# fc2 by seven block products in both halves of the tokens, from the first half's 7th group on

## The chip, the cores and the metric

One core of one Trainium2 chip runs the whole kernel. The metric is device time in microseconds (us), the median of several runs. Five engines matter: PE (TensorE) multiplies matrices, DVE (VectorE), ACT (ScalarE) and POOL (GpSimd) do elementwise work, SP (SyncE) issues the DMA transfers. Each engine works off its own instructions strictly in the order in which the program emits them.

## The reference

A transformer block on 2048 tokens of width D = 576, with an adaptive modulation (`sa, ca, ga, sb, cb, gb`) computed from a small vector `c`. Only its second half is touched by the change:

```python
x = x + ga * attention(layernorm(x) * (1 + ca) + sa)        # 32 query heads, one key/value head
h = layernorm(x) * (1 + cb) + sb
y = layernorm(h)                                            # the "second norm" of the MLP
x = x + gb * (gelu(y @ w1 + b1) @ w2 + b2)                  # w1: 576 x 4608, w2: 4608 x 576
```

All arithmetic is float32. The kernel gets it from float32r matmuls: each operand is split in a high part (a rounded copy) and a low part (operand minus high part), and a product is high times high, high times low, low times high.

## The kernel before

The attention runs first and ends at about 1430 us. Then the MLP runs in 36 *groups*, numbered v = 0 to 35 in the code's loop `for v in range(NV)`. A group takes 256 of the 4608 hidden channels for half of the tokens: v = 0 to 17 are the first *pair* of token blocks (tokens 0 to 1023), v = 18 to 35 the second pair (tokens 1024 to 2047). Tiles are 128 tokens; `XT[:, t, :]` is the residual of tile t, which is also the accumulator of the output.

In each group, fc1 is done by seven block products in the manner of Strassen and Winograd (`product`, L1042: A11, S2, S3, A12, S1, A22, S4, in this order). Each has its weights in `W1["r"]` and its input pieces in `OP`, which `op_pieces` forms from the normed and transposed activations `YR[pair]`. Weight sums for the groups that aren't precomputed (3 to 16) are formed during the first pair by `w1_part`, `w1_sum` and `tail_parts`, one group ahead, mostly on POOL, then saved to DRAM for the second pair.

fc1 gives four activation blocks per group. `gelu` (L1057) evaluates each on ACT, makes the high part on ACT (L1060) and the low part on POOL (L1061). The order in a group is A22, A11, A21, A12 in the names that fc2 uses for them; A21 is not split when fc2 goes by seven products.

fc2 differs between the pairs.

- First pair (`fc2`, L1153): 96 matmuls of 128x288 per group, 12 for each of 8 token tiles, and one DVE addition into `XT` per tile (L1157).
- Second pair, groups 18 to 34 (`fc2s`, L1122): seven block products, 12 matmuls each, 84 in all, in the order of `SEVEN`: S3, A22, A11, A12, S2, S1, S4. `sums` forms S3, S2, S1, S4 from the gelu results on POOL (L1098 the difference, L1095 the high part, L1096 the low part). Each product is followed by two DVE additions (L1128), into `XT` or into a spare accumulator `eb`, which POOL adds in at the end (L1136). The last group, 35, is plain.

fc2 of group v runs while fc1 of group v+1 does, one product between two fc1 products (`t_()` steps the generator). In the seven-product groups there are seven such places per group; the first place after the boundary holds the last product (S4) of the group before last, and S3 of the last group has the second place, behind fc1's A11 and S2. Only in the first group after the switch is the first place left out.

At the end of a group the program emits, in this order: fc1's S4 and its DVE addition (L1299); the last gelu's activation; one fc2 product with its two DVE additions; the weight sum S4 and `tail_parts` (L773 to L776, POOL) where weights are formed; then the first step of `sums`, which makes S3. After the boundary: fc1's A11, the ACT copy of it to `U` (L1230), then the last gelu's split (L1060, L1061), then the second step of `sums`, and so on.

The second norm of token blocks 2 and 3 (`ln2_tile`, eight tiles) is spread in small steps over groups 2 to 16 of the first pair (`more`, at seven places in each group).

Of the kernel before, what the change touches and what calls it, by code (L numbers as in the profile page):

```python
# [18 lines left out]
KD = 5  # L19
# [4 lines left out]
NG = F // 256  # L24
R3 = 3 * DH
# [5 lines left out]
def block_kernel(ctx: ExitStack, tc, x, wqkv, wo, w1, b1, w2, b2, c, wmod, ident_in, out):  # L31
# [34 lines left out]
    w2sum = dr.tile([NG, 128, 4, 2, 288], F32, name="w2sum")  # L66
    qscr = dr.tile([NB, 2, H * DH, TB], F32, name="qscr")
# [453 lines left out]
    def ln2_tile(tb, t):  # L521
# [15 lines left out]
        e = po if fine else ve  # L537
        e.tensor_scalar(h, X, mv[:, 0:1], rs, op0=ALU.subtract, op1=ALU.mult)
# [16 lines left out]
        if fine:
            yield
# [17 lines left out]
    def ln2_block(tb):  # L574
        if "b" not in B2:
            B2["b"] = b2_scaled(load_b2())
        if tb % 2 == 0:
            YR[tb // 2] = per.tile([128, 2 * KD, TB], F32, name="yr", tag="big", bufs=3)
        for t in range(NT):
            yield from ln2_tile(tb, t)  # L580
        if tb % 2:
            R = YR[tb // 2]
            po.tensor_tensor(R[:, 5:7], R[:, 7:9], R[:, 5:7], op=ALU.subtract)
            yield
            po.tensor_tensor(R[:, 5:7], R[:, 5:7], R[:, 0:2], op=ALU.add)
            yield
# [100 lines left out]
    def weight_parts():  # L687
# [283 lines left out]
    W2, W2S, GT = [], [], []  # L971

    def wo_end():
# [8 lines left out]
        W1["pool"] = tc.tile_pool(name="mr", bufs=1, reuse_waits="tile")  # L982
        mr = W1["pool"].__enter__()
# [3 lines left out]
        load_w2(0)  # L987

# [19 lines left out]
    def w1_sum(w):  # L1008

        o, a = W1["s"], 4 * OPS.index(w)  # L1010
        def op(x, y, how=ALU.subtract):
            po.tensor_tensor(o, x, y, op=how)
# [9 lines left out]
        po.tensor_copy(W1["r"][:, a:a + 2], o)  # L1022
# [3 lines left out]

    def load_w2(v, to=None):
        for l in range(2):
            sy.dma_start((to or W2[v % 2])[l].bitcast(F32), w2scr[v % NG, :, l])
# [14 lines left out]

    G = {(-2, 1, 0): 0, (-1, 0, 0): 1, (-1, 0, 1): 2, (-1, 1, 1): 3, (-1, 1, 0): 4}

    def gelu(v, f, b, p):

        if v < NG:
# [3 lines left out]
        else:  # L1053
            u = G[v, b, f] = GU["A%d%d" % (2 - b, 2 - f)][v % 2] if v == NV - 1 or (b, f) != (0, 1) else None
            h = YR[1][:, 2 * b + f, :]
        ft = 2 * (v % NG) + f
# [16 lines left out]
    def xb(b, nn, j):  # L1073

        return XT[:, 2 * NT + NT * (1 - b) + 2 * j:, 288 * nn:288 * (nn + 1)][:, :2]

    def eb(j):
# [9 lines left out]

    def sums(v):

        h = [[YR[1][:, 3 - 2 * i - j, :] for j in range(2)] for i in range(2)]  # L1090
        s1, s2, s3 = (YR[1][:, i, :] for i in (4, 5, 6))

        def parts(w, x):
            u = GU[w][v % 2]
            po.tensor_copy(unit(u, 0), x)  # L1095
            po.tensor_tensor(unit(u, 1), x, unit(u, 0).bitcast(F32), op=ALU.subtract)  # L1096

        po.tensor_tensor(s3, h[0][0], h[1][0], op=ALU.subtract)  # L1098
        parts("S3", s3)
        yield  # L1100
        po.tensor_tensor(s1, h[1][0], h[1][1], op=ALU.add)
        po.tensor_tensor(s2, s1, h[0][0], op=ALU.subtract)
# [4 lines left out]
        po.tensor_tensor(s3, h[0][1], s2, op=ALU.subtract)  # L1107
        parts("S4", s3)

    def fc2s(v):  # L1110

        bank = []
        for k, (w, first, to) in enumerate(SEVEN):
            gh, gl = (unit(GU[w][v % 2], l) for l in range(2))
            for j in range(2):
# [8 lines left out]
                o = eb(j) if to is None else xb(*to, j)  # L1124
                if v == NG and k == 2:
# [3 lines left out]
            if v + 2 < NV:  # L1129
                load_w2s((v + 1) % NG, k)  # L1130
            else:
                if k == 3:
                    load_w2(NV - 1, W2[0])
                for to in ((), (), (), (), ((1, 0),), ((1, 1),), ((0, 1),))[k]:
                    for j in range(2):
                        po.tensor_tensor(xb(*to, j), xb(*to, j), eb(j), op=ALU.add)  # L1136
# [3 lines left out]
    def fc2(v):  # L1140
        h2, l2 = W2[v % 2 if v < NG else 0]
        for bt in range(2 * NT):
# [15 lines left out]
            if v % NG == NG - 1:  # L1158
# [3 lines left out]
    fill = deque([ln2_block(2), ln2_block(3)])  # L1162
# [17 lines left out]
    mark = [None]  # L1180

    for v in range(NV):
        nxt = (v + 1) % NG
        if v == NG - 1:
            while fill:
                step(fill)
            form = op_pieces(YR[1], po)

        def more(half="", first="", room=False):
# [3 lines left out]
            elif 1 < v < NG and fill and (room or mark[0] != "T") and half not in ("-T3 -B21", "=T4 +t0"):  # L1193
                mark[0] = next(fill[0], "end")
                if mark[0] == "end":
                    fill.popleft()
# [15 lines left out]
        if v == NG:  # L1212
            W1["pool"].__exit__(None, None, None)
            g2 = ctx.enter_context(tc.tile_pool(name="g2", bufs=1, reuse_waits="tile"))
            g2 = g2.tile([128, 4, TB], F32R, name="gt2")
            GT.extend([g2[:, i] for i in range(4)] + [px.tile([128, TB], F32R, name="gt3", tag="gx", bufs=2)
                                                      for _ in range(2)])
            spare = ({0, 1, 2, 3, 4} - {G[v - 1, b, f] for b in range(2) for f in range(2)}).pop()
            GU.update({"A11": (5, 5), "A22": (6, 7)})
            for w, u in zip(("S3", "A21", "S1", "S2", "A12", "S4"),  # L1220
                            [spare, spare] + [G[v - 1, b, f] for b in range(2) for f in range(2)]):
                GU[w] = u, u
            for k in range(4):
# [7 lines left out]
        g_()  # L1231
        s_()
        more("+B11", "+T4")
        if v > NG + 1:
# [49 lines left out]
        w_("A22")  # L1284
        ve.tensor_tensor(bc, bc, U[:, 0], op=ALU.add)
# [80 lines left out]
```

## Time and profile before

| | |
|---|---|
| median of 3 runs | 2295.25 us (2294.14 to 2295.88) |
| the profiled execution | 2296.59 us, of which the span of the profile is 2294.8 us |
| busy share of the span | PE 99%, DVE 73%, ACT 65%, POOL 59% |
| attention and what stands before it | to 1429.7 us |
| MLP, first pair (v = 0 to 17) | 1429.7 to 1864.2 us |
| MLP, second pair (v = 18 to 35) | 1864.2 us to the end |

A group of the profile's instructions is named by line, engine, operation, and out<-in tiles. A busy time per stretch counts how long the engine had an instruction in work. In a timeline the columns are start, duration, engine, line, operation, tiles, shapes, count, and in brackets idle time before it and what ended it; several like instructions in a row are merged, and PE's durations overlap, as matmuls are pipelined.

### The profile page before, as it was taken

What the parts mean: (1) busy time and instruction counts of PE and PEld (TensorE: products, weight loads), DVE (VectorE), ACT (ScalarE), POOL (GpSimd) and SP (SyncE); (2) the same over time, 40 slices, a digit from 0 to 9 for tenths busy, and PEclk for the clock granted to TensorE, in tenths of its full rate; (3) what the DMA queues carried; (4) which work ended last, traced back from release to release, by engine and by line L of the source; (5) the groups of instructions that cost most, each with busy time, mean ns of one, the idle gap of its engine ahead of it and who ended that gap; (6) DMA issues with size and microseconds to landing.
All of it is one profiled execution on the core that took longest, in us unless ns stands there. A gap on an engine that the chain in (4) does not pass through costs nothing.

```text
span 2294.8 us, 44582 instructions
## 1 busy us (share of the span) xinstructions
PE 2260.5 (99%) x16310; PEld 1415.6 (62%) x16310; DVE 1686.0 (73%) x3004; ACT 1486.3 (65%) x2851; POOL 1350.8 (59%) x1554
## 2 busy tenths in 40 slices
PE   8999999999999999999999999999999999999999
PEld 6644443454444454444454335899999998989998
DVE  6589999978999979999879982444444456666665
ACT  5569999978999969999979998322222232222221
POOL 6634555443665425557326352588888767677776
PEclk9999999999999999999999999999999999999999
DMA  6221223222222212222223333444444456666663
GB/s 221 86 101 48 71 89 97 86 69 65 86 76 77 83 50 89 76 75 85 66 69 105 100 104 97 163 158 163 154 157 164 147 173 188 184 177 182 178 182 124
DMA packets 160412, 267.74 MB, mean 117 GB/s; under 512 B 26955, under 2 KB 67787, under 8 KB 160193
## 3 DMA queue, kind: packets, MB, share of 16 engines
q1 hardware_dynamic: 160193, 264.89, 36.7%
q8 instruction: 129, 2.11, 0.4%
q14 instruction: 90, 0.74, 0.1%
HBM read 163.45 MB, written 92.24 MB: 111 GB/s over the span
## 4 chain that ended last, share of the span: by engine, by line
PE 88%; ACT 2%; POOL 1%; issue 1%; DMA 1%; SPq 1%; DVE 0%; ACTq 0%; POOLq 0%
PE psC L813 22%; PE psB L1042 18%; PE psB L824 11%; PE psA L1153 11%; PE psM L322 9%; PE psA L1122 8%; PE psB L834 4%; PE psB L597 2%; ACT P L826 2%; ACT O L619 1%; PE psA L597 1%; PE psB L152 0%; PE psB L251 0%; DMA big<-os 0%; DMA w1scr<-r 0%
## 5 line engine op out<-in xcount | busy, mean ns | idle before, releaser
L826 ACT ACTIVATE P<-psB 128x512 f32<-128x512 f32 x2048 | 1049.1, 617 | 3.6 <-PE psB L824 1.8
L846 DVE TENSOR_REDUCE mx<-psM 128x1 f32<-128x512 f32 x1476 | 946.3, 683 | 70.0 <-PE psM L322 31.6
L813 PE MATMUL psC<-P,V 128*32 128x256 f32 (+1 forms) x6056 | 598.1, 466 | 13.4 <-ACT O L619 13.4
L824 PE MATMUL psB<-qst,KS 64*128 64x512 f32 x2048 | 597.3, 434 | 1.5 <-DMA qst<-ms 1.5
L322 PE MATMUL psM<-KS,qst 64*128 64x512 f32 x1722 | 591.2, 432 | 0.0
L824 PEld LDWEIGHTS psB<-qst,KS 64*128 64x128 f32 x2048 | 300.9, 184 | 169.8 <-issue 72.5
L1042 PE MATMUL psB<-ops,w1a 128*128 128x512 f32 x1512 | 390.5, 396 | 0.0
L322 PEld LDWEIGHTS psM<-KS,qst 64*128 64x128 f32 x1722 | 283.3, 185 | 115.1 <-DVE mx L844 93.5
L1042 PEld LDWEIGHTS psB<-ops,w1a 128*128 128x128 f32 x1512 | 271.6, 188 | 47.7
L813 PEld LDWEIGHTS psC<-P,V 128*32 128x32 f32 x6056 | 119.6, 108 | 236.4 <-issue 211.6
L1153 PE MATMUL psA<-w2s,big 128*128 128x288 f32 x1488 | 255.4, 295 | 0.0
L1057 ACT ACTIVATE yr<-psB,b1t 128x512 f32<-128x512 f32 x72 | 49.6, 689 | 287.2 <-PE psB L1042 147.1
L1153 PEld LDWEIGHTS psA<-w2s,big 128*128 128x128 f32 x1488 | 221.3, 188 | 6.7
L837 ACT ACTIVATE xc<-psB 128x512 f32<-128x512 f32 x246 | 147.5, 600 | 90.3 <-PE psM L322 68.3
L1157 DVE TENSOR_TENSOR XT<-psA,XT 128x576 f32<-128x576 f32 x152 | 114.3, 752 | 121.4 <-PE psA L1153 121.3
L1057 ACT ACTIVATE gx<-psB,b1t 128x512 f32<-128x512 f32 x72 | 49.6, 688 | 225.8 <-PE psB L1042 76.5
L844 DVE CUSTOM_DVE_ANT_0 xc<-psM,xc 128x512 f32<-128x512 f32 x246 | 167.3, 680 | 1.2 <-PE psM L322 0.6
L1128 DVE TENSOR_TENSOR XT<-psA,XT 128x576 f32<-128x576 f32 x170 | 128.8, 758 | 32.7 <-PE psA L1122 23.5
L834 PEld LDWEIGHTS psB<-KD,qst 64*128 64x128 f32 x246 | 45.1, 183 | 158.6 <-ACT P L826 109.2
L1061 POOL TENSOR_TENSOR big<-gx,big 128x512 fp32r<-128x512 f32 x72 | 94.8, 1316 | 62.7 <-ACT big L1060 46.7
L834 PE MATMUL psB<-KD,qst 64*128 64x512 f32 x246 | 122.4, 497 | 0.0
L132 POOL MEMSET qst<- 32x1024 f32 x62 | 58.6, 946 | 107.5 <-PE psM L322 47.4
(197 smaller groups left out, 2981.8 us busy)
## 6 DMA issues: line engine op xcount, KB each, us to landing
w1a<-w1scr SPq DMA_DIRECT2D x154, 256.0 KB
w1scr<-w1a SPq DMA_DIRECT2D x98, 256.0 KB
w2scr<-r SPq DMA_DIRECT2D x72, 288.0 KB
w2sum<-r SPq DMA_DIRECT2D x68, 288.0 KB
w2s<-w2sum SPq DMA_DIRECT2D x68, 288.0 KB
w2s<-w2scr SPq DMA_DIRECT2D x29, 576.0 KB
qst<-qscr SPq DMA_DIRECT2D x192, 72.0 KB
w2s<-w2scr SPq DMA_DIRECT2D x34, 288.0 KB
```

The costliest lines, as they stand in the source:

```text
L322: pe.matmul(o, QST[n][64 * g:64 * g + 64, p, 128 * qt:128 * (qt + 1)], KS[64 * g:64 * g + 64, 512 * kb:512 * (kb + 1)], start=True, stop=True)
L813: pe.matmul(PVt[n][32 * j:32 * (j + 1), cs], V[:, kc, :], t[:, j, cs], start=(kc == 0 and h0 == 0), stop=(kc == 15), skip_group_check=True)
L824: pe.matmul(t, KS[64 * g:64 * g + 64, 128 * kc:128 * (kc + 1)], QST[n][64 * g:64 * g + 64, i, :], start=True, stop=True)
L826: ac.activation(P[n, kc][:, 2 * i + g, :], t, AF.Exp, scale=SCALE)
L834: pe.matmul(t, QST[n][64 * g:64 * g + 64, p, 128 * qt:128 * (qt + 1)], KD1[64 * g:64 * g + 64, :], start=True, stop=True)
L837: ac.activation(XC[-1], t, AF.Relu)
L844: ve.tensor_tensor_reduce(c, t, c, 1.0, -3.0e38, ALU.add, ALU.max, o)
L846: ve.tensor_reduce(o, t, axis=AX.X, op=ALU.max)
L1042: pe.matmul(o, x, y, start=(first and i == 0), stop=(i == len(terms) - 1), skip_group_check=True)
L1122: pe.matmul(p[:, i, :288], x[:, ts_], W2S[k][:, y], start=(bool(first) and q == 0), stop=(q == 2), skip_group_check=True)
L1128: ve.tensor_tensor(o, p[:, :, :288], o, op=ALU.add)
L1153: pe.matmul(p[:, nn, :288], x, y, start=(q == 0), stop=(q == len(terms) - 1))
```

## The change

From group 6 (`VS`) on, the first pair too does fc2 by seven products. Groups 6 to 17 use `fc2s` and `sums`. For that, gelu results of these groups need six 512-wide buffers: they are put on the residual rows of tokens 1024 to 2047 in `XT` (`HX`), so the six tiles that lie there are first written to DRAM (`xscr`) and read back in group 18. Because of this, the second norm of blocks 2 and 3 must be over before group 6: `ln2_late` does it in groups 1 to 5, in all seven places of each group, for both blocks at once, three steps apart. In the first pair `sums` takes DVE for the sums, ACT for the high parts, POOL for the low parts, with the low part put off to the next `g_()`. The weight sums S1 and S3 move from POOL to DVE, all four high copies of weight sums from POOL to ACT. The second pair goes through the weight groups in the order 1, 2, ..., 17, 0, so that group 0 is the plain one and the precomputed `w2sum` is needed for 1 to 17 rather than 0 to 16. The first pair's output tiles are stored in groups 20 and 21.

```diff
+VS = 6
+NPK = 6
+    xscr = dr.tile([NPK, 128, D], F32, name="xscr")
...
+    def ln2_late(tb):
+        for _ in range(3 * (tb % 2)):
+            yield
+        for t in range(NT):
+            X = XT[:, NT * tb + t, :]
...
+            rs, nb = stats(X)
+            yield
+            Z = ZB[0].tile([128, 640], F32, name="Z%d" % tb)
+            h = Z[:, :D]
+            ac.activation(h, X, AF.Identity, scale=rs, bias=nb)
+            ve.tensor_tensor(X, X, B2["b"], op=ALU.add)
+            yield
+            ve.tensor_tensor(h, h, BC[:, 1, :], op=ALU.mult)
+            po.tensor_tensor(h, h, BC[:, 0, :], op=ALU.add)
+            k = NT * (tb - 2) + t
+            if k < NPK:
+                sy.dma_start(xscr[k], X)
+            yield
+            rs, nb = stats(h)
+            yield
+            ac.activation(h, h, AF.Identity, scale=rs, bias=nb)
+            ac.activation(Z[:, D:], Z[:, 512:D], AF.Copy)
+            yield
+            p = psA()
+            for k in range(KD):
+                tr(p[:, k // 4, 128 * (k % 4):128 * (k % 4 + 1)], Z, k)
...
-            po.tensor_tensor(o, x, y, op=how)
+            (ve if w in ("S1", "S3") else po).tensor_tensor(o, x, y, op=how)
...
-        po.tensor_copy(W1["r"][:, a:a + 2], o)
+        ac.activation(W1["r"][:, a:a + 2], o, AF.Copy)
...
+    HX = XT[:, 2 * NT:, :].rearrange("p a b -> p (a b)")
+    def hs(v, i):
+        return YR[1][:, i, :] if v >= NG else HX[:, TB * i:TB * (i + 1)]
...
+    def low(u, x):
+        po.tensor_tensor(unit(u, 1), x, unit(u, 0).bitcast(F32), op=ALU.subtract)
+        yield
...
     def sums(v):
+        h = [[hs(v, 3 - 2 * i - j) for j in range(2)] for i in range(2)]
+        s1, s2, s3 = (hs(v, i) for i in (4, 3, 5))
+        e = ve if v < NG else po
         def parts(w, x):
+            if v < NG:
+                ac.activation(unit(u, 0), x, AF.Copy)
+                gens.append(low(u, x))
+            else:
+                po.tensor_copy(unit(u, 0), x)
+                list(low(u, x))
+        e.tensor_tensor(s3, h[0][0], h[1][0], op=ALU.subtract)
         parts("S3", s3)
         yield
+        e.tensor_tensor(s1, h[1][0], h[1][1], op=ALU.add)
+        e.tensor_tensor(s2, s1, h[0][0], op=ALU.subtract)
         parts("S2", s2)
...
-                for to in ((), (), (), (), ((1, 0),), ((1, 1),), ((0, 1),))[k]:
+            if v in (NG - 1, NV - 2):
+                for to in ((), (), (), (), ((1, 0),), ((1, 1),), ((0, 1),))[k]:
...
+        if v == NG:
+            for k in range(NPK):
+                sy.dma_start(XT[:, 2 * NT + k, :], xscr[k])
...
-        if NG <= v < NV - 1:
+        if VS <= v < NV - 1:
             sm.append(sums(v))
             s_()
             f2.append(fc2s(v))
```

More of the change, by code (lines that the diff above doesn't have):

```diff
@@ L577, in ln2_block @@
         if tb % 2 == 0:
-            YR[tb // 2] = per.tile([128, 2 * KD, TB], F32, name="yr", tag="big", bufs=3)
+            new_yr(tb // 2)
         for t in range(NT):
@@ L987, in wo_end @@
         load_w2(0)
+        ZB.append(tc.tile_pool(name="zb", bufs=1, reuse_waits="tile"))
+        ZB[:] = ZB[0].__enter__(), ZB[0]
     def raw_w1(i):
@@ L1071, in block_kernel, with xb, eb @@
     GU = {}
-    def xb(b, nn, j):
-        return XT[:, 2 * NT + NT * (1 - b) + 2 * j:, 288 * nn:288 * (nn + 1)][:, :2]
-    def eb(j):
+    def xb(pair, b, nn, j):
+        return XT[:, NT * (2 * pair + 1 - b) + 2 * j:, 288 * nn:288 * (nn + 1)][:, :2]
+    def eb(pair, j):
+        if not pair:
+            return EB[j]
         return YR[1][:, 7:10, :].rearrange("p a b -> p (a b)")[:, :4 * 288].rearrange("p (t c) -> p t c", c=288)[
@@ L1106, in sums @@
         yield
-        po.tensor_tensor(s3, h[0][1], s2, op=ALU.subtract)
+        e.tensor_tensor(s3, h[0][1], s2, op=ALU.subtract)
         parts("S4", s3)
     def fc2s(v):
-        bank = []
+        bank, pair = [], v // NG
         for k, (w, first, to) in enumerate(SEVEN):
-            gh, gl = (unit(GU[w][v % 2], l) for l in range(2))
+            gh, gl = (unit(GU[w], l) for l in range(2))
             for j in range(2):
@@ L1123, in fc2s @@
                                   skip_group_check=True)
-                o = eb(j) if to is None else xb(*to, j)
-                if v == NG and k == 2:
+                o = eb(pair, j) if to is None else xb(pair, *to, j)
+                if v in (VS, NG) and k == 2:
                     ve.tensor_copy(o, p[:, :, :288])
@@ L1157, in fc2 @@
             ve.tensor_tensor(Xv, p[:, :, :288], Xv, op=ALU.add)
-            if v % NG == NG - 1:
+            if v == NV - 1:
                 sy.dma_start(out[128 * tt:128 * (tt + 1), :], X)
             yield
-    fill = deque([ln2_block(2), ln2_block(3)])
+    late, t1 = [ln2_late(2), ln2_late(3)], deque([t1_less(1)])
+    outs = deque(range(2 * NT))
     f2 = deque()
@@ L1192, in more @@
                 form(first if v == 0 else half if v == NG - 1 else {"+T4": "-T4 +T1 -B22", "-T4": "-T1 -t1"}.get(first, ""))
[L1193 to L1196, printed above, removed]
+            elif 0 < v < VS:
+                if not late:
+                    step(t1)
+                for s in late[:]:
+                    if next(s, 0) == 0:
+                        late.remove(s)
+            elif v in (NG + 2, NG + 3) and outs:
+                tt = outs.popleft()
+                sy.dma_start(out[128 * tt:128 * (tt + 1), :], XT[:, tt, :])
             if v == 0 and rest:
@@ L1231, in block_kernel @@
         g_()
+        if v == VS:
+            GT.extend(px.tile([128, TB], F32R, name="gt3", tag="gx", bufs=2) for _ in range(2))
         s_()
         more("+B11", "+T4")
-        if v > NG + 1:
+        if v > VS + 1:
             t_()
```

114 lines of the change are left out of this document (56 added, 58 removed).

## The prediction

> **What bounds the kernel now.** I read the page first: the busy shares, then the chain that ended last. PE is busy for 99% of the span and carries 88% of the chain, so only fewer matmuls, or matmuls that wait, can change the time.
>
> ```profile
> PE 2260.5 (99%) x16310; PEld 1415.6 (62%) x16310; DVE 1686.0 (73%) x3004; ACT 1486.3 (65%) x2851; POOL 1350.8 (59%) x1554
> PE 88%; ACT 2%; POOL 1%; issue 1%; DMA 1%; SPq 1%; DVE 0%; ACTq 0%; POOLq 0%
> ```
>
> Then I cut the MLP into its groups with the view of busy time per stretch. The rows are: two plain groups (8, without transposes, and 9, with five), group 17, group 18, group 19 (12 matmuls short), and group 25 with seven products.
>
> ```profile
> core 0: us, PE busy (x) PEld busy (x) DVE busy (x) ACT busy (x) POOL busy (x), PEclk, DMA share, GB/s
> 1617.70:1642.00 24.30, 24.30 (x148) 22.02 (x147) 12.62 (x21) 6.36 (x11) 22.30 (x31) 1.00 0.45 160
> 1642.00:1667.00 25.00, 25.00 (x154) 22.62 (x153) 10.07 (x15) 6.96 (x12) 20.04 (x28) 1.00 0.44 155
> 1839.70:1864.20 24.50, 24.50 (x150) 22.22 (x148) 16.93 (x19) 12.20 (x17) 18.41 (x9) 1.00 0.42 133
> 1864.20:1888.50 24.30, 24.30 (x148) 22.02 (x147) 11.55 (x14) 6.97 (x11) 14.09 (x10) 1.00 0.63 206
> 1888.50:1909.80 21.30, 21.30 (x125) 19.03 (x124) 12.46 (x17) 5.09 (x8) 16.41 (x15) 1.00 0.73 224
> 2024.00:2046.85 22.85, 22.85 (x136) 20.59 (x135) 14.08 (x20) 5.13 (x9) 16.45 (x16) 1.00 0.65 180
> ```
>
> PE is busy all through each of them, at full clock: both kinds of group are as long as their matmuls. A plain group takes 24.30 us, one with seven products 22.85. So 1.45 us per group is to be had where PE stays fed, and the question is whether the first pair can feed it. For that I read the timeline around a boundary between two seven-product groups (25 and 26; fc1 of group 26 begins at 2046.85).
>
> ```profile
> 2043.57 1.30 POOL L1098 TENSOR_TENSOR yr<-yr 128x512 f32<-128x512 f32 x1 [1.51 <-ACT yr L1057]
> 2045.27 1.75 PE L1122 MATMUL psA<-w2s,big 128*128 128x288 f32 x12
> 2045.63 1.29 POOL L1096 TENSOR_TENSOR big<-yr,big 128x512 fp32r<-128x512 f32 x1
> 2046.26 1.55 DVE L1128 TENSOR_TENSOR XT<-psA,XT 128x576 f32<-128x576 f32 x2
> 2046.26 0.69 ACT L1057 ACTIVATE yr<-psB,b1t 128x512 f32<-128x512 f32 x1 [2.83 <-DVE psB L1299]
> 2046.85 1.56 PE L1042 MATMUL psB<-ops,w1a 128*128 128x512 f32 x6
> 2048.25 1.78 PE L1122 MATMUL psA<-w1a,big 128*128 128x288 f32 x12
> 2048.45 0.60 ACT L1230 ACTIVATE u<-psB 128x512 f32<-128x512 f32 x1 [1.50 <-PE psB L1042]
> 2048.95 0.62 ACT L1060 ACTIVATE big<-yr 128x512 fp32r<-128x512 f32 x1
> 2049.65 1.30 POOL L1061 TENSOR_TENSOR big<-yr,big 128x512 fp32r<-128x512 f32 x1 [2.72 <-ACT big L1060]
> 2049.87 1.56 PE L1042 MATMUL psB<-ops,w1a 128*128 128x512 f32 x6
> 2051.27 1.75 PE L1122 MATMUL psA<-w2s,big 128*128 128x288 f32 x12
> ```
>
> The last row is fc2's product S3 of group 25. Twelve matmuls in 1.75 us are 0.133 apart, and its third one already reads the low part of S3: at 2051.53, which is 4.7 us after the boundary. POOL made the difference at 2043.57, as soon as the third gelu was there, and ended the low part at 2046.92 (2045.63 + 1.29). There are 4.6 us to spare.
>
> **The change part by part.** *Matmuls removed.* Twelve groups (6 to 17) lose 12 of 96 matmuls each: 12 x 1.45 = 17.4 us less, if nothing waits. The fc2 of a group runs in the next, so the gain falls into groups 7 to 18, with group 7 short as group 19 is now.
>
> *S3 in the first pair comes later.* This is the term that decides. The program emits S3's difference after the two DVE additions of the group's last fc2 product, and it is now on DVE. So in the frame of the rows above: DVE is free at 2047.81 and takes about 0.65 for it (half of the 1.21 of a 128x1024 difference, quoted below), to 2048.5. The high part on ACT (0.62, as L1060) goes to 2049.2. The low part waits for the next g_(), so ahead of it in order stand the copy to U (0.60, to 2049.8) and the last gelu's high part (to 2050.3) on ACT, and on POOL that gelu's low part (1.30, to 2051.7). S3's low part then ends at 2052.95 and PE goes on at about 2053.05, where it wanted to at 2051.53: a wait of 1.5 us, more than the 1.45 gained. Behind the waiting matmul stands all of PE's queue; the chain restarts from PE at the next boundary, so the wait comes back each time.
>
> *POOL's own work ahead of it.* In groups 7 to 15 the weight sum S4 and the tails of the next weights are emitted before S3. In the plain group 9 they run like this, from the low part of S4 to the last tail:
>
> ```profile
> 1665.54 0.74 POOL L1023 TENSOR_TENSOR w1a<-w1s,w1a 128x256 fp32r<-128x256 f32 x1
> ...
> 1668.30 0.47 POOL L776 TENSOR_TENSOR w1a<-w1d,w1a 64x128 fp32r<-64x128 f32 x1
> ```
>
> That is 3.23 us. S4's high copy goes to ACT behind the last gelu (over at 2046.95, plus 0.4 for the copy), so the low part starts at 2047.4 and the tails end at 2050.6; the two low parts behind them end at 2053.2: a wait of 1.7 by this path. And here DVE and POOL meet. Rows of group 17, where DVE forms fc1's pieces from two tiles in SBUF while POOL works:
>
> ```profile
> 1845.03 1.46 DVE L929 TENSOR_TENSOR ops<-yr,ops 128x1024 fp32r<-128x1024 f32 x1
> 1845.36 2.29 POOL L1061 TENSOR_TENSOR big<-gx,big 128x512 fp32r<-128x512 f32 x1
> 1845.44 1.06 ACT L927 ACTIVATE ops<-yr 128x1024 fp32r<-128x1024 f32 x1 [2.00 <-POOL yr L585]
> 1847.01 1.72 DVE L929 TENSOR_TENSOR ops<-yr,ops 128x1024 fp32r<-128x1024 f32 x1
> 1848.66 1.21 DVE L920 TENSOR_TENSOR yr<-yr 128x1024 f32<-128x1024 f32 x1
> 1857.12 1.30 POOL L1061 TENSOR_TENSOR big<-gx,big 128x512 fp32r<-128x512 f32 x1
> 1857.19 2.31 DVE L920 TENSOR_TENSOR yr<-yr 128x1024 f32<-128x1024 f32 x1 [0.35 <-POOL ops L929]
> ```
>
> The same DVE difference takes 1.21 with POOL idle and 2.31 when it begins just behind a POOL subtract, and ends 1.08 after that subtract does. The POOL subtract takes 2.29 rather than 1.30 when DVE was first: 0.99 lost to a 1024-wide difference, so 0.5 to a 512-wide one. In the new order S3's, S1's and S2's differences all come on DVE within two microseconds of the boundary, in the middle of POOL's tails: 3 x 0.5 on top of 1.7 is 3.2. Ends 1.5 and 3.2; I take 3.0, near the upper end, as each such meeting in the rows costs the wait, and a little under it, as not each meets the start of a POOL instruction. Nine boundaries (into groups 8 to 16): 27.0 us.
>
> The Trainium skill ("SBUF — State Buffer", Who interferes with whom) says that a DVE instruction with two SBUF inputs contends with a GpSimd instruction that reads SBUF, by an exclusive lock. The trace agrees (2.31 against 1.21, 2.29 against 1.30). By that rule the sum is the one below; if the engines did not meet, the nine waits would be 1.5 and the sum 13.5 lower.
>
> *Into group 7* the first fc2 place is missing, as in group 19 now:
>
> ```profile
> 1888.50 2.97 PE L1042 MATMUL psB<-ops,w1a 128*128 128x512 f32 x12
> 1891.31 1.75 PE L1122 MATMUL psA<-w2s,big 128*128 128x288 f32 x12
> ```
>
> S3's low part is wanted 3.1 us after the boundary, 1.6 earlier. In return group 6 still ends with two plain products behind fc1's S4, so POOL's tails are 1.6 further on. Between 6.2 and 6.6 after the boundary: a wait of 3.4.
>
> *Group 17* takes seven products and forms fc1's pieces for the second pair. Into it: no weights are formed, 1.5. Within: the three DVE forms quoted (1.46 + 1.72 + 1.21 = 4.4) stand between the additions of S3's and A22's products; there is one pair of accumulators ahead, and the product after (A11) needs the pair that the additions for A22 free. By the order, about 2 us of wait; ends 0 and 4.
>
> *Into group 18*: ACT has three more high copies of pieces ahead of S3's (two of 1.06 and one of half that, 2.7 in all, of which 1.1 fall into time in which ACT would wait for the difference), so S3's chain is 1.6 later than the 1.5: 3.1. *Into group 19*: POOL adds the spare accumulator, two pairs of 128x576 ahead of S3's sum:
>
> ```profile
> L1136 POOL TENSOR_TENSOR XT<-XT,yr 128x576 f32<-128x576 f32 x6 | 8.4, 1442 | 1.6 <-DVE yr L1128 1.6
> ```
>
> Two of 1.44 lie between the product's end and the sum: S3 of group 18 is ready 6.4 after the boundary instead of 4.7 at the latest: 1.8, ends 0 and 2.5.
>
> *The norm in groups 1 to 5* moves 2.3 tiles into a group that had half of one. Transposes: as many, in the same rows (25.00 against 24.30 for five). What it may cost is PE waiting for a transpose's input or for the accumulators that it shares with fc2. DVE would be busy some 20 of 25 us; no row shows such a density, today's costs no wait. Ends 0 and 8 (1 us per tile); I take 2.
>
> *At nothing.* POOL in groups 6 to 15: mean 21.2, less 2.6 of norm (half a tile's three 128x576 instructions, 1.44 each, and small ones), less 3.1 of weight work (two sums of 0.74, four copies of some 0.4), plus three low parts (3 x 1.30), is 19.4 of over 22.85; it is late at the boundary, not full. DMA: second-layer blocks as in the second pair, loaded a whole group ahead; at 180 GB/s that pair runs without a wait. The parked tiles: 6 x 0.29 MB out in groups 1 to 4; back in group 18, where SP stands until the last low part of group 17 is made (about 20 us in); 1.8 MB at 206 to 224 GB/s land some 3 us into group 19, ahead of the first addition that needs them; loads queued behind have a group to spare (without that cover: up to 2 us). The order of the weight groups and the outputs' new place move nothing on PE. The second pair's S2 now lies on a gelu buffer, but there POOL makes sums in order, 3 us before that gelu writes.
>
> *Sum.* Waits: 3.4 + 27.0 + 1.5 + 2.0 + 3.1 + 1.8 + 2.0 = 40.8; less 17.4: +23.4 us on the profiled span of 2294.8, so 2318.2. The profiled execution took 2296.59, 1.8 more than its span and 1.3 more than the median 2295.25. On the median: 2318.7, say 2318.
>
> **The rivals.** *No meeting of DVE and POOL at the boundary*: waits of 1.5 set by the ACT chain alone; 2318 - 13.5 = 2305. For it: POOL has gaps between its short tails; against: the rows above.
>
> *Faster: S3's low part is in time.* If POOL takes it right behind its high part (2049.2 + 1.3 = 2050.5), before the tails and the last gelu's part, PE wanted it only at 2051.53. Then only groups 17 to 19 and the norm still wait (2.0 + 1.6 + 1.8 + 2.0): 2295 - 17.4 + 7.4 = 2285. It decides where the nine waits average under (17.4 - 13.8) / 9 = 0.4 us. For it: the second pair has 4.6 us to spare; against: the order in which low parts are emitted. *About the same:* the low part overtakes the last gelu's but not the tails, ending at 2051.9, a wait of 0.4: 2295.
>
> *The clock falls.* The one stretch in which PE runs dry, between projections and attention, shows this:
>
> ```profile
> 124.40:127.80 3.40, 2.69 (x12) 1.53 (x11) 2.58 (x3) 0.61 (x2) 1.19 (x1) 1.00 0.36 118
> 127.80:131.20 3.40, 1.44 (x6) 0.57 (x6) 2.64 (x3) 0.61 (x2) 1.27 (x1) 1.00 0.28 91
> 131.20:138.00 6.80, 6.78 (x27) 5.25 (x27) 5.12 (x8) 2.75 (x6) 0.00 (x0) 0.50 0.46 129
> ```
>
> A stretch of 3.4 us with 1.44 busy is followed by 6.8 us at half clock, which costs 3.4 us of work. A wait of 3 us could do that at each of ten boundaries: up to 2318 + 34 = 2352, at half of them 2335. Against: PE is dense on both sides. The Trainium skill ("TensorE: Matmul & The Clock Gate", Part 1) halves the clock after an idle window of about 3.4 us; by that, waits of 3.0 don't trip it and 2318 stands, but the row with 1.44 busy did, so it keeps a chance.
>
> **How the numbers follow.** Forecast as summed 0.40 (its own range 2308 to 2328), no meeting 0.16, clock 0.12, the norm's visits far denser than thought (up to 2330) 0.04: slower 0.72. In time: 0.18. The same: 0.10. What a measurement tells from no change is 0.2%, 4.6 us. The range reaches from the faster case's 2286 to half of the clock's, 2336; it leaves out the lower half of the first and the upper half of the second, and tails.
>
> **What would show it.** Right: groups 8 to 16 last 25 to 26 us with PE idle some 3 us once in each, at the third matmul of fc2's S3, released by POOL's low part in `low`; POOL's tails stretched beside DVE's sums. If groups 8 to 16 last 22.9 us, the faster rival holds; at 24.4 the one without a meeting; PEclk below 1.00 there shows the clock. Wrong above all would be my order of S3's low part on POOL, on which 27 of the 41 us hang.

## The result, and the profile after

The change makes the kernel slower: 2350.28 us, median of six runs (2348.53 to 2352.42), against 2295.57 for the kernel before beside it (2294.14 to 2297.57); ratio 1.0238, interval 1.0224 to 1.0251. The direction was forecast, the size was not: 2350 lies outside the range of 2286 to 2336. One execution of experiment 1 below, at a mean granted clock of 0.675 where its others had 0.995, took 2859.88 us and is left out of its median.

The profiled span is 2346.7 us, 51.9 more than before. The page's busy shares and its chain of waits, shares by engine:

```profile
PE 2268.5 (97%) x16166; PEld 1415.5 (60%) x16166; DVE 1787.6 (76%) x3144; ACT 1540.3 (66%) x2967; POOL 1358.6 (58%) x1512
PE 83%; POOL 4%; ACT 4%; DVE 2%; issue 1%; SPq 0%; DMA 0%; ACTq 0%; POOLq 0%; DVEq 0%
```

PE has 144 matmuls fewer (the twelve groups' 12 each) and is busy for *longer*, 2268.5 against 2260.5 us. Fewer matmuls in more busy time means that some of them ran slower. Busy time per stretch, with the columns as before, shows where: groups 1 to 5 together, group 3 alone, then groups 7, 10, 17 and one of the second pair, 25.

```profile
1442.10:1587.80 145.70, 133.58 (x772) 117.84 (x771) 80.49 (x145) 56.53 (x103) 99.26 (x136) 0.96 0.41 142
1497.70:1535.30 37.60, 31.26 (x163) 27.14 (x162) 19.14 (x36) 15.00 (x28) 25.31 (x38) 0.86 0.37 126
1612.10:1637.80 25.70, 22.86 (x124) 20.31 (x123) 16.66 (x23) 9.15 (x18) 18.80 (x21) 0.93 0.59 181
1692.30:1719.60 27.30, 24.64 (x136) 22.05 (x135) 18.38 (x26) 9.63 (x20) 20.49 (x22) 0.94 0.57 173
1883.40:1911.90 28.50, 23.86 (x136) 20.70 (x135) 22.52 (x29) 11.60 (x19) 14.85 (x10) 0.99 0.55 156
2076.60:2099.40 22.80, 22.80 (x135) 20.54 (x135) 14.06 (x20) 5.11 (x9) 16.44 (x16) 1.00 0.63 179
```

Groups 8 to 16 are all like group 10: 27.3 us, where a seven-product group that waits for nothing takes 22.8. In group 10 PE is idle for 27.30 - 24.64 = 2.66 us and at a mean clock of 0.94. The waits of PE in groups 7 to 16 (columns: line, what it waited for, us in all, times, longest) have one entry:

```profile
PE psA L1183 <- POOL big L1141: 26.8, 10, 2.8
```

L1183 is the matmul of `fc2s`, L1141 the subtract in `low`. The timeline around the boundary from group 10 to 11 (at 1719.6) shows the chain on which the forecast rested:

```profile
1720.04 0.75 POOL L1064 TENSOR_TENSOR w1a<-w1s,w1a 128x256 fp32r<-128x256 f32 x1 [0.71 <-ACT w1a L1063]
1720.49 0.84 DVE L1159 TENSOR_TENSOR XT<-XT 128x512 f32<-128x512 f32 x1
...
1721.26 0.95 DVE L1162 TENSOR_TENSOR XT<-XT 128x512 f32<-128x512 f32 x1
1721.37 0.63 ACT L1153 ACTIVATE big<-XT 128x512 fp32r<-128x512 f32 x1 [1.41 <-DVE XT L1159]
...
1722.54 1.07 POOL L816 TENSOR_TENSOR w1a<-w1r,w1a 64x256 fp32r<-64x256 f32 x1
...
1724.03 0.42 PE L1183 MATMUL psA<-w2s,big 128*128 128x288 f32 x2
1724.05 0.46 POOL L816 TENSOR_TENSOR w1a<-w1d,w1a 64x128 fp32r<-64x128 f32 x1
1724.59 1.26 POOL L1111 TENSOR_TENSOR big<-XT,big 128x512 fp32r<-128x512 f32 x1
1725.81 2.51 POOL L1141 TENSOR_TENSOR big<-XT,big 128x512 fp32r<-128x512 f32 x2
1727.12 1.09 PE L1183 MATMUL psA<-w2s,big 128*128 128x288 f32 x3 [2.67 <-POOL big L1141]
```

S3's difference (L1159) begins 0.9 us after the boundary, its high part (L1153) is there at 1722.0, and its low part is the first of the last row but one's two subtracts, behind the tails and the last gelu's low part: it ends at 1727.07. PE does two matmuls of S3 and waits 2.67 us for the third. From the first row to the end of the last L816 POOL needs 4.47 us, where the same instructions took 3.23 before.

Cut finer, into the three 3.41 us stretches around the same wait in the group before (its PE resumes at 1699.8):

```profile
1696.39:1699.80 3.41, 0.79 (x5) 0.45 (x3) 1.32 (x2) 0.00 (x0) 3.25 (x5) 1.00 0.68 219
1699.80:1703.21 3.41, 3.37 (x12) 3.23 (x13) 1.33 (x2) 0.65 (x2) 2.80 (x4) 0.50 0.19 68
1703.21:1706.63 3.42, 3.42 (x21) 3.08 (x20) 2.30 (x4) 0.29 (x1) 1.85 (x2) 1.00 0.72 220
```

After the wait the clock is 0.50 for 3.41 us, 12 matmuls where 21 fit afterwards. Such a stretch loses 1.7 us of work, and one follows every wait in groups 7 to 16. In the whole MLP 47.8 us run at half clock, 23.9 us of work lost.

In groups 1 to 4, where the norm is done, the two longest entries of the waits are these:

```profile
PE psA L155 <- ACT Z L617: 5.7, 3, 2.3
PE psA L1214 <- DVE XT L1218: 5.3, 4, 2.0
```

L155 are the norm's transposes, L1214 the plain `fc2`, whose accumulators DVE frees in L1218. One of them, in group 2, by the timeline:

```profile
1481.96 0.87 ACT L617 ACTIVATE Z<-Z,st,st 128x576 f32<-128x576 f32 x1 [1.09 <-POOL st L152]
1483.27 0.87 ACT L606 ACTIVATE Z<-XT,st,st 128x576 f32<-128x576 f32 x1
1484.17 0.76 DVE L607 TENSOR_TENSOR XT<-XT,b2g 128x576 f32<-128x576 f32 x1 [3.72 <-ACT Z L606]
1484.84 0.75 DVE L1218 TENSOR_TENSOR XT<-psA,XT 128x576 f32<-128x576 f32 x1
1485.65 0.40 PE L1214 MATMUL psA<-w2s,big 128*128 128x288 f32 x1 [2.00 <-DVE XT L1218]
```

One block's step on ACT waits for POOL's small statistics; the other block's step (L606) stands behind it; the bias addition (L607) waits for that on DVE, because it overwrites what L606 reads; fc2's addition stands behind L607; PE waits for it. Three engines in strict order, two blocks interleaved: each hands on the other's delay.

### The profile page after: what moved, and what is told of

Its sections match the earlier page's. It is cut to its first block, busy times and chain, and to the rows that moved or that the text cites. A ratio compares the mean times of both kernels' runs of the same rounds, so it can differ in the third digit from the quotient of the medians.

```text
span 2346.7 us, 44729 instructions
## 1 busy us (share of the span) xinstructions
PE 2268.5 (97%) x16166; PEld 1415.5 (60%) x16166; DVE 1787.6 (76%) x3144; ACT 1540.3 (66%) x2967; POOL 1358.6 (58%) x1512
## 4 chain that ended last, share of the span: by engine, by line
PE 83%; POOL 4%; ACT 4%; DVE 2%; issue 1%; SPq 0%; DMA 0%; ACTq 0%; POOLq 0%; DVEq 0%
PE psC L853 23%; PE psB L1086 15%; PE psA L1183 13%; PE psB L864 12%; PE psM L325 10%; PE psB L874 4%; PE psA L1214 3%; PE psB L637 2%; ACT P L866 2%; POOL big L1111 1%; POOL big L1141 1%; POOL w1a L816 1%; ACT O L659 1%; PE psA L637 1%; POOL w1a L815 0%
## 5 line engine op out<-in xcount | busy, mean ns | idle before, releaser
L1086 PE MATMUL psB<-ops,w1a 128*128 128x512 f32 x1512 | 399.8, 401 | 0.0
L1086 PEld LDWEIGHTS psB<-ops,w1a 128*128 128x128 f32 x1512 | 277.3, 192 | 47.3
L1189 DVE TENSOR_TENSOR XT<-psA,XT 128x576 f32<-128x576 f32 x290 | 218.3, 756 | 85.5 <-PE psA L1183 71.9
L1183 PE MATMUL psA<-w2s,big 128*128 128x288 f32 x1392 | 218.7, 307 | 32.7 <-POOL big L1141 29.4
L1183 PEld LDWEIGHTS psA<-w2s,big 128*128 128x128 f32 x1392 | 207.7, 198 | 46.9 <-POOL big L1141 32.4
L734 POOL CAST r<-w2b 128x288 fp32r<-128x288 f32 x104 | 44.3, 426 | 118.4 <-DMA w2scr<-r 66.5
L1063 ACT ACTIVATE w1a<-w1s 128x256 fp32r<-128x256 f32 x56 | 23.3, 416 | 123.6 <-POOL w1s L1053 83.7
L1183 PE MATMUL psA<-w2s,gt 128*128 128x288 f32 x696 | 102.7, 297 | 1.3 <-DVE XT L1189 1.3
```

The source lines that it names most:

```text
L1086: pe.matmul(o, x, y, start=(first and i == 0), stop=(i == len(terms) - 1), skip_group_check=True)
L1183: pe.matmul(p[:, i, :288], x[:, ts_], W2S[k][:, y], start=(bool(first) and q == 0), stop=(q == 2), skip_group_check=True)
L1189: ve.tensor_tensor(o, p[:, :, :288], o, op=ALU.add)
```

## The experiments

Line numbers shift by up to seven where an edit adds or removes lines. All edits are to the changed kernel. Ratios are to the kernel before, run alongside.

**1. S3 made earlier.** Does the wait vanish when S3's chain starts before the boundary?

```diff
         if v <= VS:
             t_()
+        if VS <= v < NG:
+            sm.append(sums(v))
+            s_()
         wt(w1_part, "A22", True)
...
-            sm.append(sums(v))
-            s_()
+            if v >= NG:
+                sm.append(sums(v))
+                s_()
```

> As the changed kernel, but in the first pair the difference S3, its high part and its low part are emitted one fc1 product earlier, right behind the fc2 product that follows the third gelu, so that the low part stands ahead of the weight sum S4, the tails and the last gelu's part on POOL. Theory A (PE waits 2.67 us per boundary for S3's low part, and each such wait brings 3.4 us of half clock, which costs another 1.7 us): the wait at S3 is gone in groups 7 to 16, they last 22.9 us at full clock instead of 27.3, and the time falls by about 9 x 4.4 + 5 = 45 us, to some 2305. Rival B (POOL, busy 20.5 us and held up by DVE, is simply full, so that the wait turns up at another product): groups 8 to 16 stay above 25.5 us, the time above 2330.

Measured: 2312.26 us, 1.0083 (1.0067 to 1.0100). No half clock in groups 7 to 16; groups 8 to 15 take 23.8 to 24.5 us. The longest of them, group 9, and the waits of groups 7 to 16:

```profile
1657.60:1682.10 24.50, 23.31 (x135) 20.30 (x135) 19.89 (x27) 9.36 (x18) 19.95 (x22) 1.00 0.61 197
PE psA L1183 <- ACT XT L1107: 6.7, 9, 1.2
```

The wait of 2.67 us is gone, and the time is 38.0 us less than the changed kernel's. What is late next is DVE: the weight sum S1, which the change put on DVE, stands ahead of two of fc2's additions.

```profile
1701.39 1.51 DVE L1053 TENSOR_TENSOR w1s<-w1r 128x256 f32<-128x256 f32 x1 [1.74 <-POOL w1a L1064]
1703.43 0.74 DVE L1189 TENSOR_TENSOR eb<-psA,eb 128x576 f32<-128x576 f32 x1
1704.27 1.83 PE L1183 MATMUL psA<-w2s,big 128*128 128x288 f32 x12 [0.53 <-ACT XT L1107]
```

The view names a gelu as releaser, but this product belongs to the group before that gelu's and doesn't read it. DVE's addition (the row before) ends at 1704.17, 0.1 us before PE goes on, and experiment 12, which moves S1 away, takes nearly all of these waits with it.

**2. The norm alone.** `VS = 18` takes the seven products out of the first pair and leaves the norm in groups 1 to 5.

```diff
-VS = 6
+VS = 18
```

> VS = 18: the norm of blocks 2 and 3 in five visits as in the changed kernel, but the whole first pair with plain fc2. Theory A (the norm's visits cost 22.7 us in groups 1 to 5, 3.8 of which are transposes that left later groups): groups 1 to 5 as in the changed kernel (145.7 us), groups 6 to 17 at 24.3 to 24.5; the time is 2295 + 19 = 2314, or 2311 if the 3.3 us by which the attention ended earlier in the changed kernel belong to the new order of the weight sums. Rival B (the visits are cheap by themselves and groups 1 to 5 suffer from something else that the seven products bring): groups 1 to 5 near 125 us, the time 2297.

Measured: 2313.12 us, 1.0082 (1.0066 to 1.0099). Groups 1 to 5 take 144.7 us, groups 6 to 17 24.32 or 24.42. Group 3, and the longest entry of the waits of groups 1 to 5:

```profile
1501.60:1537.10 35.50, 29.49 (x163) 25.75 (x162) 19.24 (x36) 15.01 (x28) 24.12 (x36) 0.90 0.37 130
PE psA L155 <- ACT Z L617: 5.3, 3, 3.3
```

So without the seven products the change still costs 19.1 us, with the same waits and with half clock. The weight sums' moves to DVE and ACT are in it too; experiment 6, which has them as well, bounds them at 3.8 us. The rest is the norm's new place.

**3. S3's low part at once**, in place of behind the last gelu's.

```diff
-                gens.append(low(u, x))
+                list(low(u, x)) if w == "S3" else gens.append(low(u, x))
```

> As the changed kernel, but S3's low part goes to POOL right behind its high part, ahead of the last gelu's low part (1.3 us). Theory A: the wait at S3 falls from 2.67 to about 1.4 us; if a wait of 1.4 no longer trips the clock, groups 8 to 16 last 24.3 us and the time is about 2322; if it still does, 26.0 and 2338. Rival B (the half clock has nothing to do with the length of the wait): half-clock stretches as many as before, groups at 26.0, 2338. Rival C (the last gelu's part is not in the way): no change, 2350.

Measured: 2317.95 us, 1.0106 (1.0091 to 1.0121). Group 9, and the waits of groups 7 to 16:

```profile
1658.00:1682.60 24.60, 23.13 (x136) 20.63 (x136) 19.47 (x26) 9.64 (x20) 20.55 (x22) 1.00 0.64 197
PE psA L1183 <- POOL big L1141: 14.4, 10, 1.5
```

The wait falls from 2.67 to 1.46, by the 1.2 of one low part. But a group falls from 27.3 to 24.6, by 2.7: the clock holds at 1.00.

**4. The wait filled with matmuls.** Twenty matmuls of 128x288 ahead of each S3 of the first pair, whose results are overwritten.

```diff
+                    for _ in range(20 if k == j == i == pair == 0 else 0):
+                        pe.matmul(p[:, i, :288], gh[:, ts_], W2S[k][:, 0], start=True, stop=True, skip_group_check=True)
                     for q, (x, y) in enumerate(((gh, 0), (gh, 1), (gl, 0))):
```

> As the changed kernel, with 20 more matmuls of 128x288 (20 x 0.133 = 2.66 us) put in front of each S3 product of the first pair, on operands that are ready; the accumulator is started afresh behind them. PE then works through the time in which it waited. Theory A (the half clock comes from PE's idle time): no half clock in groups 7 to 17, groups 8 to 16 last 22.85 + 2.7 = 25.6 us instead of 27.3, and the time falls by 9 x 1.7 + 2 = 17 us, to about 2333, though PE does 220 matmuls more. Rival B (the rows of half clock are a matter of the records, the matmuls that follow are not slowed): 27.3 us per group as before, 2350. Rival C (the added matmuls only come on top, the wait stays behind them): 29.9 us per group, 2376.

Measured: 2335.67 us, 1.0183 (1.0168 to 1.0198): 14.6 us *less* than the changed kernel, with 240 matmuls more (12 places, the one into group 18 among them). Group 9:

```profile
1662.90:1688.80 25.90, 25.79 (x156) 23.30 (x155) 18.62 (x26) 9.63 (x20) 20.58 (x22) 1.00 0.60 188
```

No wait over 0.3 us and no half clock in groups 7 to 16. The balance, roughly: 240 x 0.133 = 31.9 us of matmuls in place of 28.5 us of waits for S3's low part in groups 7 to 18, less ten half-clock stretches of 1.7, less 0.9 by which groups 2 and 3 differ, is -14.6, the difference of the medians; the MLP of the two profiled executions differs by 12.9. This parts the clock from the wait: S3 is no earlier here.

**5. The bias addition last** in the norm's steps, and the tile's store with it, so that DVE doesn't wait for ACT there; `VS = 18` besides.

```diff
-            ve.tensor_tensor(X, X, B2["b"], op=ALU.add)
...
             ve.tensor_copy(yr[:, 4], p[:, 1, :128])
+            ve.tensor_tensor(X, X, B2["b"], op=ALU.add)
...
```

> As the norm alone in five visits (plain fc2 in the whole first pair), but DVE's addition of the bias to the residual tile, which overwrites what ACT reads, and the tile's store move from the step of ACT's first pass to the last step. Theory A (DVE stands still until ACT has read the tile, ACT until POOL's small instructions of the statistics, and the additions that free fc2's accumulators stand behind DVE's wait): the waits of PE at the accumulators (1.25, 1.99 and 1.74 us in groups 1 to 3) go, those at the transposes stay; groups 1 to 5 last about 138 us instead of 144.7, the time is some 2306. Rival B (the transposes' input is the only thing that counts): 144 us, 2313.

Measured: 2308.65 us, 1.0061 (1.0046 to 1.0076); groups 1 to 5 take 141.8 us rather than 144.7. The waits for accumulators behind L1218 fall from 5.3 to 2.2 us; those of the transposes rise from 5.3 to 6.5. So the chain shown for group 2 is a real part, but the smaller one.

**6. The norm at half the pace**, the two blocks in turns, in groups 1 to 9; `VS = 18`.

```diff
+    turn = deque(late)
...
+                turn.rotate()
...
-                    if next(s, 0) == 0:
+                    if s is turn[0] and next(s, 0) == 0:
```

> As the norm alone (plain fc2 in the whole first pair), but the two blocks take turns, one step at each place, so that the visits reach from group 1 to 9 and every step has twice the time. Theory A (the steps are too close: each step's chain over DVE, POOL and ACT is longer than the way to the next place): hardly a wait in groups 1 to 9, which last 9 x 24.4 + 5.1 = 225 us; the time is that of the kernel before, 2294 to 2297. Rival B (the work of the visits itself is too much for some engine): the loss stays at about 18 us, 2312.

Measured over ten runs: 2298.61 us, 1.0017 (1.0007 to 1.0026). Group 6 is the longest:

```profile
1567.90:1595.10 27.20, 25.77 (x158) 23.16 (x157) 14.58 (x26) 10.69 (x21) 21.58 (x30) 1.00 0.47 164
```

Three waits are left, 3.5 us in all, and no half clock. Of the 19 us, density makes 15.

**7. The weight sums' high copies back on POOL**; `VS = 18`.

```diff
-        ac.activation(W1["r"][:, a:a + 2], o, AF.Copy)
+        po.tensor_copy(W1["r"][:, a:a + 2], o)
```

> As the norm alone in five visits (plain fc2 in the whole first pair), with the four high copies of the weight sums back on POOL. Theory A (ACT's copies wait for POOL's weight sums, and the norm's ACT passes, which feed the transposes, stand behind them): PE's waits at the transposes (0.70, 3.26 and 1.35 us) shrink by half or more, groups 1 to 5 last 139 us instead of 144.7, the time is some 2307. Rival B (POOL is the late one in any case, and gets 1.6 us more per group): no better, 2313 to 2318.

Measured: 2311.34 us, 1.0071 (1.0055 to 1.0088); groups 1 to 5 143.2 us. The transposes' waits fall from 5.3 to 3.5 us, the accumulators' rise from 6.3 to 7.7. So it was not time on ACT alone that the norm lacked.

**8. The sums S1 and S2 later**, away from POOL's tails.

```diff
         ac.activation(U[:, 0], ba, AF.Copy)
         g_()
...
-        s_()
+        if not VS < v <= NG:
+            s_()
...
         s_()
+        if VS < v <= NG:
+            s_()
```

> As the changed kernel, but in groups 7 to 18 the second step of the sums (DVE's differences S1 and S2, the high part of S2) comes one fc1 product and one fc2 product later, so that of DVE's three differences only S3's falls into POOL's tails. Theory A (DVE and POOL hold each other up there, 0.5 us for each of the two): the wait at S3 falls from 2.67 to about 1.7 us; if the clock then holds, as it did with a wait of 1.46, groups 8 to 16 last 24.6 us and the time is about 2325; if not, 26.3 and 2341. Rival B (no meeting; the chain over ACT sets the wait): 2.67 and 27.3 as before, 2350.

Measured: 2343.67 us, 1.0212 (1.0197 to 1.0228). The tails at one boundary, first and last:

```profile
1665.06 0.74 POOL L1064 TENSOR_TENSOR w1a<-w1s,w1a 128x256 fp32r<-128x256 f32 x1 [0.56 <-ACT w1a L1063]
...
1668.29 0.46 POOL L816 TENSOR_TENSOR w1a<-w1d,w1a 64x128 fp32r<-64x128 f32 x1
```

They take 3.69 us, not 4.47, and six of the nine waits are 1.9: 0.77 shorter. So these two DVE instructions had lengthened POOL's tails, by 0.8 us. (Groups 17 and 18 become 4.2 us longer here, which takes back a part of the gain.) Groups 9 and 10 have the same wait, and differ:

```profile
1664.60:1691.20 26.60, 24.70 (x136) 21.89 (x135) 18.72 (x26) 9.64 (x20) 20.29 (x22) 0.94 0.60 182
1691.20:1716.20 25.00, 23.09 (x136) 20.51 (x135) 18.57 (x26) 9.59 (x19) 20.04 (x22) 1.00 0.61 190
```

In group 9 the idle time lies in one stretch of 3.41 us, and the next is at half clock; in group 10 it is split over two, 0.53 and 1.37, and nothing follows:

```profile
1669.28:1672.70 3.42, 1.52 (x12) 1.32 (x11) 1.17 (x2) 0.00 (x0) 2.79 (x3) 1.00 0.74 266
1672.70:1676.11 3.41, 3.41 (x12) 2.83 (x11) 1.46 (x3) 0.42 (x1) 1.46 (x2) 0.50 0.53 152
...
1693.18:1696.59 3.41, 2.88 (x17) 2.37 (x16) 2.20 (x3) 1.42 (x3) 3.11 (x6) 1.00 0.87 299
1696.59:1700.00 3.41, 2.04 (x13) 1.95 (x14) 1.16 (x3) 0.00 (x0) 2.79 (x4) 1.00 0.57 202
1700.00:1703.42 3.42, 3.42 (x22) 3.06 (x21) 2.33 (x5) 0.42 (x1) 0.74 (x2) 1.00 0.72 222
```

**9 to 11. Looking for a version that gains.** All three have the norm at half the pace and therefore `VS = 10` (eight groups, 11.6 us to be had), and the early S3 of experiment 1. The first also has the bias addition last and all weight sums on POOL:

```diff
-            (ve if w in ("S1", "S3") else po).tensor_tensor(o, x, y, op=how)
+            po.tensor_tensor(o, x, y, op=how)
```

> A version meant to win: seven products from group 10 on (VS = 10) instead of 6, the norm's two blocks taking turns over groups 1 to 9, the bias addition in the norm's last step, S3 emitted early as in the run that did so, all weight sums on POOL. Theory A (only S3's lateness, the half clock it brings, and the density of the norm made the change slow): group 11 at 21.3 us, 12 to 16 near 22.9 at full clock, groups 17 to 19 still 77 us (DVE's forms, POOL's additions) against 70 before, groups 1 to 9 up to 3 us over 225: 2295 - 10 + 7 + 0 to 3 = 2292 to 2295. Rival B (POOL, with the weight sums back, is too full for the seven products): groups 12 to 15 above 24 us, the time above 2300.

Measured: 2323.18 us, 1.0122 (1.0106 to 1.0137). New waits of 3.9, 1.2, 2.4, 1.2 and 2.4 us in groups 12 to 16; before the first, the timeline has

```profile
1732.64 0.73 POOL L1053 TENSOR_TENSOR w1s<-w1r 128x256 f32<-128x256 f32 x1
1733.40 0.42 ACT L1063 ACTIVATE w1a<-w1s 128x256 fp32r<-128x256 f32 x1 [2.81 <-POOL w1s L1053]
1733.72 0.67 ACT L1107 ACTIVATE XT<-psB,b1t 128x512 f32<-128x512 f32 x1
1734.50 0.69 DVE L1159 TENSOR_TENSOR XT<-XT 128x512 f32<-128x512 f32 x1 [5.85 <-ACT XT L1107]
1735.71 1.41 DVE L1189 TENSOR_TENSOR XT<-psA,XT 128x576 f32<-128x576 f32 x2
```

The weight sum is late on POOL, its copy blocks ACT, the gelu waits behind the copy, S3's difference waits for the gelu on DVE, and fc2's additions stand behind the difference. Two waits of 6.2 and 5.5 us came in groups 6 and 7 besides, behind the norm.

The second adds two moves: DVE copies the norm's transposes out, and forms B21's low part.

```diff
-            ac.activation(yr[:, :4], p[:, 0].rearrange("p (k c) -> p k c", k=4), AF.Copy)
+            ve.tensor_copy(yr[:, :4], p[:, 0].rearrange("p (k c) -> p k c", k=4))
...
-        at = {"B11": (0, 0, ve), "B21": (2, 2, e2), ...
+        at = {"B11": (0, 0, ve), "B21": (2, 2, ve), ...
```

> As the version before it, and besides the transposes of the norm are copied out of PSUM by DVE alone, and B21's low part, for which DVE's difference T4 waits in group 17, is made by DVE instead of POOL. Theory A: no waits at the accumulators that the transposes share with fc2 (groups 1 to 9 at 225 us), and group 17 some 2.5 us shorter: 2288 to 2292, 0.2% faster than the kernel before. Rival B (DVE, busy 16 us in such groups, is then the late one): no better than the version before it.

Measured: 2310.85 us, 1.0069 (1.0057 to 1.0082). The long waits in groups 6 and 7 are gone (one of 2.1 in group 8 is left, with half clock behind it), and group 17 falls from 27.4 to 26.0 us; groups 12 to 16 keep the new waits (1.4 to 2.9).

The third keeps these two moves, puts the bias addition back in its place and the weight sums S1 and S3 back on DVE, with S1 emitted behind S3's difference:

```diff
-        wt(w1_sum, "S1")
+        if v < VS:
+            wt(w1_sum, "S1")
...
+        if VS <= v < NG:
+            sm.append(sums(v))
+            s_()
+            wt(w1_sum, "S1")
```

> VS = 10 and the norm's blocks taking turns, S3 early, the weight sums S1 and S3 on DVE as in the changed kernel, but S1's behind S3's difference instead of ahead of fc1's A22; the norm's transposes copied out by DVE; B21's low part on DVE. Theory A (what was left in the run with S3 early, 0.5 to 1.2 us per group, came from DVE holding fc2's additions up while it made the weight sum S1 beside POOL; and the weight sums on POOL made the last two runs slow): groups 12 to 16 near 23.0 us at full clock, groups 1 to 9 at 226, 17 to 19 at 75.5: 2292. Rival B (the waits only move to the next additions): groups 12 to 16 at 23.8 or more, 2296 or more.

Measured over eleven runs: 2295.20 us against 2294.28, 1.0004 (0.9995 to 1.0013): no difference. No half clock in the MLP. The longest entries of PE's waits from group 1 to 19:

```profile
PE psA L1183 <- issue: 3.4, 6, 1.4
PE psA L1183 <- DVE XT L1189: 1.2, 1, 1.2
PE psA L1183 <- ACT big L1153: 1.1, 1, 1.1
```

The first entry is five waits of 0.4 in groups 12 to 16 and one of 1.42 in group 17. Groups 12 to 16 take 23.7 to 23.9 us, less than half the gain; groups 17, 18 and 19 take 26.0, 24.9 and 24.7; the norm keeps 1.9 us of waits. Nothing is left of the 11.6.

**12. Experiment 1 with S1 behind S3's difference**, nothing else.

> The changed kernel (VS = 6, five visits) with S3 early and the weight sum S1 behind S3's difference. Theory A: groups 8 to 15 fall from 23.8 to 24.5 us in the run with S3 early to 23.0, the time from 2313 to about 2305, and what is left against the kernel before is the norm's 19 us and groups 17 to 19. Rival B: no change, 2313.

Measured: 2312.07 us, 1.0075 (1.0062 to 1.0088), against 2312.26: no difference in time. The waits behind DVE's weight sum are gone as meant but for two of 0.2 us, group 7 falls from 22.6 to 21.2; in their place stand the 0.4 us "issue" waits, and group 17 takes 28.1 rather than 27.6.

## Why the prediction was right in sign and wrong in size

Each term of its sum against the lengths of the groups (a group's length less that of one that waits for nothing: 22.83, or 21.23 with a place missing):

| term | predicted | measured | of it half clock |
|---|---|---|---|
| matmuls removed | -17.4 | -17.9 | |
| into group 7 | 3.4 | 4.5 | 1.7 |
| nine boundaries into 8 to 16 | 27.0 | 40.1 | 15.4 |
| group 17, into it and within | 3.5 | 5.7 | |
| into 18 | 3.1 | 3.0 | 1.7 |
| into 19 | 1.8 | 1.8 | |
| norm in groups 1 to 5 | 2.0 | 18.9 | 5.1 |
| sum | 23.4 | 56.1 | 23.9 |

The matmuls removed are twelve groups of 24.32 - 22.83. The norm's 18.9 is 22.7 by which groups 1 to 5 are longer, less 3.8 for six tiles' transposes that left later groups. The MLP grew by 55.2, as groups 20 to 35 became 0.8 shorter besides; its first matmul came 3.3 us earlier (1426.4 rather than 1429.7), so the span grew by 51.9.

That the term into 18 agrees is in part chance. It was meant as one wait of 3.1 for S3; there is 0.57 of wait for S3's low part in that group, 0.62 elsewhere, and 1.7 of half clock, which the wait at the end of group 17 brought on. The low part is ready 6.67 us after the boundary, so at full clock PE, which wants it 4.68 after, would have waited for some 2.0 (an estimate from these rows).

*Right: the chain of S3.* "S3 in the first pair comes later. This is the term that decides." The wait sits at S3's third matmul, released by POOL's low part, 2.67 us where 3.0 was said. What it is made of is shown too: experiment 1 moves S3's whole chain ahead of POOL's tails, and the wait is gone; experiment 3 takes the last gelu's low part from ahead, and the wait falls by 1.2; experiment 8 takes two of the three DVE sums off POOL's tails, and it falls by 0.77. The forecast had 3 x 0.5 for this meeting; the tails grew by 4.47 - 3.23 = 1.24. The Trainium skill ("SBUF — State Buffer", Who interferes with whom) says that a DVE instruction with two SBUF inputs and a GpSimd instruction that reads SBUF contend; these runs agree (4.47 us beside three such sums, 3.69 beside one).

*The term for group 17* was mis-sized: "By the order, about 2 us of wait; ends 0 and 4" for the DVE forms came to 0.70 and 2.81, inside its ends. The trace labels the second "issue"; DVE's sum of pieces (L960) runs 1906.99 to 1909.26, after waiting 2.48 for POOL, and the additions that free the accumulators stand behind it. When experiment 10 formed B21's low part on DVE, the wait fell to 1.42.

*Wrong, step one: the clock.* The rival "The clock falls" got a chance of 0.12 and no place in the sum. That its "up to 2318 + 34 = 2352" is near the measured time is luck: it took 3.4 us for each of ten boundaries, and the runs show 1.7; the norm made up the difference. The drop came at every boundary into groups 7 to 16, where it cost 17.1 us, and experiment 4 shows that it was the clock: with the wait filled, PE does more and is done sooner. The sentence that failed is "by that, waits of 3.0 don't trip it and 2318 stands". The page cited there ("TensorE: Matmul & The Clock Gate", Part 1, the Trainium skill) speaks of an idle window of about 3.4 us. The runs differ: 1.9 us of idle time within one stretch of 3.41 is enough. The prediction had quoted the row that said so, 3.40 us with 1.44 busy, and then let the rule outweigh it. "Against: PE is dense on both sides" was no argument either: in group 10, PE is busy all through the stretch after the half-clock one, and the clock falls at the next wait all the same.

*Wrong, step two: the norm.* "Ends 0 and 8 (1 us per tile); I take 2" measured 18.9, beyond the upper end. The prediction looked at how busy DVE would be, some 20 of 25 us. DVE was busy for 15 to 19 us in each of groups 1 to 4, no more than that, and yet late: what counts is the order. Experiment 5 (DVE's wait for ACT removed) and experiment 7 (ACT relieved) gave back 2.9 and 1.5 us of groups 1 to 5 and moved the waits elsewhere; experiment 6, which halves the pace, gave back 15 of 19, the half clock with them. The waits bunch in group 3, 37.6 us long; why there, no run shows.

With these two as measured the sum comes to 2318 + 17.1 + 16.9 = 2352. *"Faster: S3's low part is in time"* was forecast at 2285 (the last but one paragraph calls it 2286) with waits of 2.0 for the norm. Experiment 1 makes that rival true, and with the norm's 18.9 the forecast for it would be 2302; it gave 2312, because the next queue, DVE with its weight sum, made PE wait for 0.5 to 1.2 us in nine groups (7 to 16 are 11 us longer than without waits), and because group 17 stayed 4.8 us too long.

What stays open: the 0.4 us waits labelled "issue" in the last versions (no experiment took them apart), and whether an order exists that keeps the gain.

## What to carry to other kernels

Before work is moved to another place or engine, write out each queue around the place where the fed engine needs its operand, and ask of each instruction what it stands behind; busy shares of 60 to 80% hide waits that recur in every iteration. Price a recurring wait on PE twice: its length, and, from about 1.9 us on, 1.7 us more of work at half clock; in these runs a wait brought under 1.8 us lost the second price at once. And when a row of the trace contradicts a rule, put the row into the sum.

## What the runs showed of the hardware

Half-clock stretches start on a fixed grid of 3.413 us: in the changed kernel ten of them begin at 1617.89, 1645.20, 1672.51, ..., 1863.65, eight steps of 3.413 apart. The groups settled into that beat (27.3 us = 8 steps): PE went on 0.28 us behind the start of the half clock at the first of these waits, 0.13 and 0.07 at the next two, and within 0.04 of it from the fourth on. Over the MLP's first 560 us in the profiles of both kernels and of the twelve experiments, PE's idle time per grid step was added up. Of the steps at full clock, each of the 51 with 1.90 us or more (1.90 to 3.41) was followed by a step at half clock, and none with 1.85 us or less was. In a step at half clock less was enough to stay there: the eight with 0.76 to 1.63 us idle were followed by another one, so that the stretch lasted 6.83 us, and the 51 with 0.56 or less were not. The idle time need not be in one piece for this, and a wait of 1.9 that straddles two steps costs only itself, as in group 10 of experiment 8. So useless matmuls, put into the waits, made the changed kernel 14.6 us faster.
